# A linear-attention and MoE-style feed-forward kernel: attention products per head, in halves of the matrix array

## The chip, the cores and the metric

The kernel runs on one core of a Trainium2 chip. The metric is the device time of one execution in microseconds, 277.82 us in the median of three runs (277.59 to 278.0). The core has five engines that run side by side and are tied together by semaphores: TensorE (PE, matrix products; its weight loads are listed apart as PEld), VectorE (DVE), ScalarE (ACT), GpSimd (POOL) and SyncE (SP). In this kernel POOL and SP mostly issue transfers.

## The reference

For each of 8 batches and 8 heads, with 576 rows and a head width of 64, the reference forms `kv = k^T v` (64 x 64), then `out = q kv`, and divides each row of a head by its root mean square and scales it by `g_norm`. The heads are laid side by side, which gives x with 4608 rows (tokens) and 512 columns. Then

```
h = x @ w_in                                  # 4608 x 2048
g = max(h, 0) + alpha * min(h, 0)
y = g @ w_out                                 # 4608 x 512
```

The result is float32. The kernel computes its products on fp16 operands with fp32 sums.

## The kernel before

The 4608 tokens are cut into nine windows of 512. The main loop (L1010) runs over windows 1 to 8, and each pass has 16 units. A unit of pass w holds, in this order on PE: one group of the first product for a block of 128 hidden columns (`m1_group`, four products 128 x 512 into one PSUM bank, L487); seven products 128 x 256 of the second product of the window before (`prod_mm`, L665); and what `attention(w + 1, u)` adds, the attention of the window after, so that x of window w + 1 is ready when pass w + 1 starts. The order of all engines is written out by hand; each engine takes its instructions in program order.

The first product's bank is read twice: ACT makes `m_sb = relu(-h)` (L494) and then DVE makes `gt` from `m_sb` and the bank (L498). In passes 2 to 8 the first product has two banks in turn, tags h1 and h2, so the group of unit u + 2 may start only when `gt` of unit u is done. DVE also makes sums and differences of `gt` blocks (`s_sum`, L603 to L609, placed by `S_ROW`), because the second product is computed from seven block products in place of eight, and adds the partial results (`y_read`: p1, u2, u3, c11, c22, c21, c12).

From window 3 (`W_ROW`) the attention runs in rows. For each batch b from 3 to 7, `step_kv` multiplies k and v of a pair of heads at once: five products with 128 weight columns and 128 moving columns give a 128 x 128 block, of which only the two 64 x 64 blocks on the diagonal belong to a head; DVE multiplies by a mask and stores fp16 (L360). Four pairs make 20 products for a batch, placed in units 0, 0, 1, 1 of a pass (2, 2, 3, 3 in pass 2). Then, for each of the four row tiles of 128 tokens in the window, `rows_mm` multiplies the transposed q of a pair (the weights, 128 x 128) with the masked kv block (128 moving columns). Four products fill one bank of 512 columns; a tile that lies across two batches takes eight. There are 24 row tiles in windows 3 to 8, three of them across two batches. ACT squares the bank (`sq`, L444), DVE sums the squares per head (`ssq`, L450), ACT makes the reciprocal root (`rs`, L459), DVE scales (`norm`, L467) and SP transposes the rows into x by a transfer (L472).

These steps have fixed units: products of the tiles after units 2, 4, 6, 8; ssq in 4, 6, 8, 10; rs and norm in 5, 7, 9, 11; all one later in pass 2 (`ATT_ROW`, L975). SP also transposes q of the next batch in units 7, 9 and 11 (`QT_AT`), and ACT regroups k of the batch after (L177). The add u3 stands ahead of unit 10 and c22 ahead of unit 12 (`R_FIRST`). PSUM has eight banks, all in use: three of tags h, one y, one s, two o, one q. The kv blocks alternate between s and o; row tiles 0, 1 and 3 use o, tile 2 uses s.

Of the kernel before, what the change touches and what calls it, by code (L numbers as in the profile page):

```python
# [9 lines left out]
FP32 = mybir.dt.float32  # L10
FP16 = mybir.dt.float16
AF = mybir.ActivationFunctionType
ALU = mybir.AluOpType
# [4 lines left out]
def kernel(  # L18
# [11 lines left out]
    nc = tc.nc  # L30

    B, H, S, D = q.shape
# [3 lines left out]
    P = 128  # L36
    NPAIR = H // 2
    W = 512
# [15 lines left out]
    const_p = ctx.enter_context(tc.tile_pool(name="constp", bufs=1))  # L54
# [4 lines left out]
    attn_p = ctx.enter_context(tc.tile_pool(name="attn", bufs=2))  # L59
# [4 lines left out]
    ps_h = ctx.enter_context(tc.tile_pool(name="psh", bufs=1, space=bass.MemoryType.PSUM))  # L64
    ps_y = ctx.enter_context(tc.tile_pool(name="psy", bufs=1, space=bass.MemoryType.PSUM))
    ps_s = ctx.enter_context(tc.tile_pool(name="pss", bufs=1, space=bass.MemoryType.PSUM))
    ps_o = ctx.enter_context(tc.tile_pool(name="pso", bufs=2, space=bass.MemoryType.PSUM))
    ps_q = ctx.enter_context(tc.tile_pool(name="psq", bufs=1, space=bass.MemoryType.PSUM))

    ctx.enter_context(  # L70
        tc.manual_schedule(engines={ENG.PE, ENG.Activation, ENG.DVE, ENG.Pool, ENG.SP})
# [5 lines left out]
    def early_pair(eng, nm, tag):  # L77
# [14 lines left out]
            name=nc.get_next_instruction_name(),  # L92
# [9 lines left out]
    mask32 = const_p.tile([P, P], FP32, name="mask32")  # L102
# [7 lines left out]
    PAD = P // 2  # L110
    qt_sb = [const_p.tile([P, NPAIR, PAD + S + PAD], FP16, name=f"qt_sb{i}") for i in range(2)]
# [6 lines left out]
    for r in range(P // D):  # L118
        nc.sync.dma_start(
            out=alpha_row[NF : NF + 1, r * D : (r + 1) * D], in_=g_norm[:].unsqueeze(0)  # L120
# [6 lines left out]
    bufs = []  # L127
    for i in range(NBUF):
        t = {}
        for nm in ("k", "v", "q") if i < 2 else ("k", "v"):  # L130
            n = 1 if nm == "v" else T0 if i == 0 else NT
# [150 lines left out]


    qts, kvs, xts = {}, {}, {}

    def rows(b):
        return P0 if b == 0 else P

    def n_runs(b):
        return T0 if b == 0 else NT  # L290

    def pair_cols(b, nm, j):
        def f(t):
            n = rows(b)
            if nm == "v" and b == 0:
                h = 2 * j % HH
                return stages[b, nm, 2 * j // HH][0:n, h : h + 2, t, :]
            if nm == "v" and t < TPP:
                return stages[b, nm][:, 2 * j : 2 * j + 2, t, :]
            if nm == "v":  # L300
                return buf_of(b, nm)[0:n, 0, 2 * j : 2 * j + 2, :]
            return buf_of(b, nm)[0:n, t, 2 * j : 2 * j + 2, :]
        return f
# [44 lines left out]
    def step_kv(b, j, pool=(ps_s, "s")):  # L348
        ks, vs = pair_cols(b, "k", j), pair_cols(b, "v", j)
        kv_ps = pool[0].tile([P, P], FP32, name="kv_ps", tag=pool[1])  # L350
        for t in range(n_runs(b)):
            nc.tensor.matmul(  # L352
                out=kv_ps[:],
                lhsT=ks(t),
                rhs=vs(t),
                start=(t == 0),
                stop=(t == n_runs(b) - 1),
            )
        kvs[b, j] = attn_p.tile([P, P], FP16, name="kv_sb", tag=f"kv{j}")
        nc.vector.tensor_mul(out=kvs[b, j][:], in0=kv_ps[:], in1=mask32[:])  # L360


    ots = {}

    def step_ot(w, j, pool=None, parts=1):
        if pool is not None:
            ot_ps = pool[0].tile([P, W], FP32, name="ot_ps", tag=pool[1])
        else:
            ot_ps = ps_o.tile([P, W], FP32, name="ot_ps", tag="o")
        n0 = w * W  # L370
        while n0 < (w + 1) * W:
            b = n0 // S
            n1 = min((b + 1) * S, (w + 1) * W, n0 + W // parts)
            nc.tensor.matmul(  # L374
                out=ot_ps[:, n0 - w * W : n1 - w * W], lhsT=kvs[b, j][:],
                rhs=qts[b, j][:, n0 - b * S : n1 - b * S], start=True, stop=True,
            )
            n0 = n1
        sq = attn_p.tile([P, W], FP16, name="sq_sb")
        for c in col_parts(parts):  # L380
            nc.scalar.activation(out=sq[:, c], in_=ot_ps[:, c], func=AF.Square)
        ots[w, j] = (ot_ps, sq)
# [34 lines left out]
            xts[w] = xt_p.tile([P, NPAIR, W], FP16, name="xt")  # L417
        return xts[w][:, j, :]

    def rows_mm(w, i):  # L420
        n0 = w * W + i * P
        b, r = divmod(n0, S)
        pool, tag = (ps_s, "s") if i == 2 else (ps_o, "o")
        o_ps = pool.tile([P, W], FP32, name="or_ps", tag=tag)
        for j in range(NPAIR):
            cols = o_ps[:, j * P : (j + 1) * P]
            if r + P <= S:
                c = PAD + r
                nc.tensor.matmul(  # L429
                    out=cols, lhsT=qt_sb[b % 2][:, j, c : c + P], rhs=kvs[b, j][:],  # L430
                    start=True, stop=True,
                )
            else:
                assert r + PAD == S
                nc.tensor.matmul(
                    out=cols, lhsT=qt_sb[b % 2][:, j, S : S + P], rhs=kvs[b, j][:],
                    start=True, stop=False,
                )
                nc.tensor.matmul(
                    out=cols, lhsT=qt_sb[(b + 1) % 2][:, j, 0:P], rhs=kvs[b + 1, j][:],  # L440
                    start=False, stop=True,
                )
        sq = attn_p.tile([P, W], FP16, name="sq_sb")
        nc.scalar.activation(out=sq[:], in_=o_ps[:], func=AF.Square)  # L444
        ots[w, "r", i] = (o_ps, sq)

    def rows_ssq(w, i):
        o_ps, sq = ots.pop((w, "r", i))
        ssq = attn_p.tile([P, H], FP32, name="ssq_r")
        nc.vector.tensor_reduce(  # L450
            out=ssq[:], in_=sq[:].rearrange("p (h d) -> p h d", h=H),
            axis=mybir.AxisListType.X, op=ALU.add,
        )
        ots[w, "r", i] = (o_ps, ssq)

    def rows_rs(w, i):
        o_ps, ssq = ots.pop((w, "r", i))
        rstd = attn_p.tile([P, H], FP32, name="rstd_r")
        nc.scalar.activation(  # L459
            out=rstd[:], in_=ssq[:], func=AF.Abs_reciprocal_sqrt, bias=eps_t[:], scale=inv_d,  # L460
        )
        ots[w, "r", i] = (o_ps, rstd)

    def rows_norm(w, i):
        o_ps, rstd = ots.pop((w, "r", i))
        xr = attn_p.tile([P, H, D], FP16, name="x_rows", tag="rstd" if i % 2 else "x_rows")
        nc.vector.tensor_tensor(  # L467
            out=xr[:], in0=o_ps[:].rearrange("p (h d) -> p h d", h=H),
            in1=rstd[:].unsqueeze(2).to_broadcast([P, H, D]), op=ALU.mult,
        )  # L470
        xt_cols(w, 0)
        nc.sync.dma_start_transpose(  # L472
            out=xts[w][:, :, i * P : (i + 1) * P], in_=xr[:].rearrange("p h d -> p (h d)"),
        )

    gts = {}
# [135 lines left out]
    part = {}  # L612
# [124 lines left out]
    Q_POOL, S_POOL, O_POOL = (ps_q, "q"), (ps_s, "s"), (ps_o, "o")  # L737
# [230 lines left out]
            ATT_1.setdefault(at, []).append((what, j))  # L968
    ATT = {"t": step_t, "kv": step_kv, "ot": step_ot, "ssq": step_ssq}

    def row_kv(w, j):
        step_kv(w, j, O_POOL if j % 2 else S_POOL)

    ATT_ROW = {}
    for first, kv_at, d in ((True, (2, 2, 3, 3), 1), (False, (0, 0, 1, 1), 0)):  # L975
        at_row = {}
        for what, ats in (
            ("kv", kv_at), ("mm", (2 + d, 4, 6, 8)), ("ssq", (4, 6, 8, 10)),
            ("rs", (5, 7, 9, 11)), ("norm", (5, 7, 9, 11)),
        ):  # L980
            for j, at in enumerate(ats):
                at_row.setdefault(at if what == "kv" else at + d, []).append((what, j))
        ATT_ROW[first] = at_row
    ROWS = {"kv": row_kv, "mm": rows_mm, "ssq": rows_ssq, "rs": rows_rs, "norm": rows_norm}
    QT_AT = {False: {7: (0,), 9: (1,), 11: (2, 3, 4)}, True: {8: (0,), 10: (1,), 12: (2, 3, 4)}}

    def attention(w, u):
        if W_ROW <= w < NW:
            for what, j in ATT_ROW[w == W_ROW].get(u, ()):
                if what != "kv" or w < B:  # L990
                    ROWS[what](w, j)
            if w + 1 < B:
                dma_t(w + 1, QT_AT[w == W_ROW].get(u, ()))
        elif w < NW:
            for what, j in (ATT_1 if w == 2 else ATT_AT).get(u, ()):
                if what == "t" and w >= B_NAT:
                    continue
                if w < B or what in ("ot", "ssq"):
                    if w == 2 and what in ("kv", "ssq"):
                        pool = Q_POOL if j % 2 == 0 else S_POOL  # L1000
                        (step_kv if what == "kv" else step_ssq)(w, j, pool)
                    else:
                        ATT[what](w, j)
# [1 line left out]
    REG_AT = {9 + 2 * j: (("k", j),) for j in range(NPAIR)}  # L1005

    Y3_AT = [(13, 13), (13, 13), (13, 13), (13, 14), (14, 14), (14, 15), (15, 15), (15, 15), (15, 15), (15, 15), (15, 15), (15, 15), (15, 15), (15, 15), (15, 16), (16, 16)]
    REG_2 = {0: (("k", 0), ("k", 1)), 1: (("k", 2),), 2: (("k", 3),)}

    for w in range(1, NW):  # L1010
        if w + 2 < B:
# [50 lines left out]
    w = NW - 1  # L1062
# [56 lines left out]
```

## Time and profile before

| | |
|---|---|
| median of three runs | 277.82 us |
| profiled execution, first to last instruction (span) | 275.2 us |
| what lies around the span, by the difference to the median | 2.6 us |
| PE, PEld, DVE, ACT, POOL busy | 269.1, 176.1, 231.2, 154.9, 86.3 us |
| TensorE clock granted | 1.000 |
| passes with row attention (2 to 7) | about 66 to 233 us of the span |

The page gives no time of the profiled execution other than its span, so the 2.6 us are the median of the runs less that span. Matrix products overlap in the array: a record of one product is its time from start to end, and the rate is read from the distance between starts. Starts in the timeline are microseconds from the start of the span.

### The profile page before, as it was taken

How to read it: one execution, taken by the hardware profiler on the slowest of the kernel's cores; microseconds unless marked ns; L12 is line 12 of the kernel's file. 1: busy time of each engine (PE TensorE's matmuls, PEld its weight loads, DVE VectorE, ACT ScalarE, POOL GpSimd, SP SyncE). 2: the span in 40 equal slices, each digit the busy share in tenths (PEclk: the TensorE clock that was granted, in tenths of full speed). 3: DMA queues.
4: the chain of work that ended last, by engine and by line, in shares of the span. 5: the costliest groups of instructions: out<-in, count | busy, mean ns of one | idle time of the engine just before them, and what ended most of it. 6: DMA issues, size and time to landing. Idle time of an engine off the chain costs nothing.

```text
span 275.2 us, 5282 instructions
## 1 busy us (share of the span) xinstructions
PE 269.1 (98%) x1973; PEld 176.1 (64%) x1973; DVE 231.2 (84%) x451; ACT 154.9 (56%) x286; POOL 86.3 (31%) x123
## 2 busy tenths in 40 slices
PE   7899999999999999999999999999999999999995
PEld 3454454555776776676667766676667666666794
DVE  6659758799789979997999799978997999887863
ACT  3568446799989746644665456645545553444210
POOL 8853463660912338127322641100111011000200
PEclk9999999999999999999999999999999999999999
DMA  8999999999999849997984799520322032201223
GB/s 160 197 203 198 197 202 189 215 132 182 129 172 129 124 91 138 174 204 100 173 155 120 114 166 175 118 87 2 76 76 79 6 83 67 76 2 38 72 84 114
DMA packets 87341, 34.53 MB, mean 125 GB/s; under 512 B 58884, under 2 KB 85652, under 8 KB 87316
## 3 DMA queue, kind: packets, MB, share of 16 engines
q0 software_dynamic: 58064, 24.35, 68.3%
q1 hardware_dynamic: 28212, 8.83, 16.9%
q10 hardware_dynamic: 1040, 1.02, 1.2%
q8 instruction: 15, 0.25, 0.4%
q14 instruction: 10, 0.08, 0.1%
HBM read 36.71 MB, written 9.44 MB: 168 GB/s over the span
## 4 chain that ended last, share of the span: by engine, by line
PE 87%; DMA 10%; POOL 1%; issue 1%; DVE 0%; POOLq 0%
PE h_ps L487 38%; PE yY L665 15%; PE yX L665 10%; PE yZ L665 10%; DMA qst<-in_q_dram 8%; PE y L519 4%; PE kv_ps L352 3%; DMA w_in_sb<-in_moe_w_in_dram 2%; PE h_ps L510 2%; PE or_ps L429 2%; PE qt_ps L308 1%; PE ssq_ps L397 1%; PE yZ L660 1%; PE ot_ps L374 1%; POOL vst L142 0%
## 5 line engine op out<-in xcount | busy, mean ns | idle before, releaser
L487 PE MATMUL h_ps<-xt,w_in_sb 128*128 128x512 f16 x544 | 136.8, 379 | 0.0
L494 ACT ACTIVATE m_sb<-h_ps 128x512 f32<-128x512 f32 x144 | 86.1, 598 | 79.8 <-PE h_ps L487 69.6
L498 DVE SCALAR_TENSOR_TENSOR gt<-m_sb,beta_sb,h_ps 128x512 f16<-128x512 f32 x144 | 106.4, 745 | 23.6 <-ACT m_sb L494 21.8
L487 PEld LDWEIGHTS <-w_in_sb 128*128 128x128 f16 x544 | 51.6, 98 | 38.9
L530 POOL DMA_DIRECT2D out_dram<-y_sb x36 | 22.6, 630 | 134.8 <-DVE y_sb L709 43.7
L665 PEld LDWEIGHTS <-s 128*128 128x128 f16 x496 | 48.5, 98 | 19.1
L665 PEld LDWEIGHTS <-gt 128*128 128x128 f16 x384 | 37.3, 98 | 14.0
L665 PE MATMUL yY<-wsum,s 128*128 128x256 f16 x256 | 36.3, 273 | 0.0
L665 PE MATMUL yX<-w_out_sb,gt 128*128 128x256 f16 x256 | 36.1, 273 | 0.0
L159 POOL DMA_DIRECT2D qst<-in_q_dram x20 | 17.7, 923 | 1.8 <-DMA vst<-in_v_dram 1.8
L665 PE MATMUL yY<-wsum,gt 128*128 128x256 f16 x128 | 17.6, 273 | 0.0
L444 ACT ACTIVATE sq_sb<-or_ps 128x512 f16<-128x512 f32 x24 | 14.3, 597 | 5.7 <-PE or_ps L429 4.6
L665 PE MATMUL yZ<-wsum,s 128*128 128x256 f16 x120 | 16.7, 273 | 0.0
L665 PE MATMUL yZ<-w_out_sb,s 128*128 128x256 f16 x120 | 16.7, 273 | 0.0
L467 DVE TENSOR_TENSOR x_rows<-or_ps,rstd_r 128x512 f16<-128x512 f32 x24 | 16.4, 685 | 0.0
L450 DVE TENSOR_REDUCE ssq_r<-sq_sb 128x8 f32<-128x512 f16 x24 | 16.3, 680 | 0.0
L519 PE MATMUL y<-w_out_sb,gt 128*128 128x512 f16 x64 | 15.9, 379 | 0.0
L605 DVE TENSOR_TENSOR s<-s,gt 128x512 f16<-128x512 f16 x32 | 13.5, 422 | 0.5
L603 DVE TENSOR_TENSOR s<-gt 128x512 f16<-128x512 f16 x32 | 13.5, 420 | 0.0
L609 DVE TENSOR_TENSOR s<-gt,s 128x512 f16<-128x512 f16 x32 | 13.3, 420 | 0.0
L697 DVE TENSOR_TENSOR u<-yY,p 128x512 f32<-128x512 f32 x16 | 11.0, 684 | 1.9 <-PE yY L665 1.7
L607 DVE TENSOR_TENSOR s<-gt 128x512 f16<-128x512 f16 x32 | 12.6, 418 | 0.0
(88 smaller groups left out, 269.9 us busy)
## 6 DMA issues: line engine op xcount, KB each, us to landing
out_dram<-y_sb POOLq DMA_DIRECT2D x16, 256.0 KB, 2.7
kst<-in_k_dram POOLq DMA_DIRECT2D x7, 512.0 KB, 7.0
vst<-in_v_dram POOLq DMA_DIRECT2D x6, 512.0 KB, 9.2
qst<-in_q_dram POOLq DMA_DIRECT2D x20, 128.0 KB, 6.8
w_out_sb<-in_moe_w_out_dram POOLq DMA_DIRECT2D x8, 256.0 KB, 11.6
out_dram<-y_sb SPq DMA_DIRECT2D x5, 256.0 KB, 2.3
w_in_sb<-in_moe_w_in_dram POOLq DMA_DIRECT2D x2, 512.0 KB, 10.6
qst<-in_q_dram POOLq DMA_DIRECT2D x2, 512.0 KB, 12.2
```

Of the source, the lines that this page charges most:

```text
L159: nc.gpsimd.dma_start(out=st[:, t, :, :], in_=srcs["q"][b, :, t * P : (t + 1) * P, :].rearrange("h p d -> p h d"),)
L444: nc.scalar.activation(out=sq[:], in_=o_ps[:], func=AF.Square)
L450: nc.vector.tensor_reduce(out=ssq[:], in_=sq[:].rearrange("p (h d) -> p h d", h=H), axis=mybir.AxisListType.X, op=ALU.add,)
L467: nc.vector.tensor_tensor(out=xr[:], in0=o_ps[:].rearrange("p (h d) -> p h d", h=H), in1=rstd[:].unsqueeze(2).to_broadcast([P, H, D]), op= ...
L487: nc.tensor.matmul(out=h_ps[:], lhsT=w_in_blk(c, g), rhs=xts[w][:, c, :], start=(c == 0), stop=(c == NC - 1),)
L494: nc.scalar.activation(out=m_sb[:], in_=h_ps[:], func=AF.Relu, scale=-1.0)
L498: nc.vector.scalar_tensor_tensor(out=gts[w, i][:, r, :], in0=m_sb[:], scalar=beta_sb[:, g : g + 1], in1=h_ps[:], op0=ALU.mult, op1=ALU.add,)
L519: nc.tensor.matmul(out=y[:], lhsT=gt_cols(w, g, a * P, (a + 1) * P), rhs=w_out_blk(g), start=(g == 0), stop=(g == NF - 1),)
L530: engs[store_turn[0] % len(engs)].dma_start(out=dst, in_=src)
L603: nc.vector.tensor_add(out=t[:], in0=a21, in1=a22)
L605: nc.vector.tensor_sub(out=t[:], in0=sums[w, 1, k][:], in1=a11)
L665: nc.tensor.matmul(out=bank, lhsT=lhs, rhs=rhs, start=fresh, stop=(c == NK - 1), skip_group_check=True,)
```

## The change

Kv products of batches 3 to 7 are formed per head. The five products of a pair become ten, each with the 64 columns of one head as weights and 64 moving columns; head 0 of the pair writes PSUM partitions 0 to 63 and head 1 partitions 64 to 127, so each uses one half of the array's columns. All four pairs of a batch go into one bank of tag s, in one run of 40 products in unit 0 (unit 2 in pass 2). Two DVE copies of 64 partitions x 256 elements replace the four masked multiplies, and write only the diagonal blocks of one of two fixed tiles `kv_masked`, whose other blocks were left zero by batches 0 to 2, which still use the masked multiply.

Row products are formed per head as well: the weights are 64 rows of transposed q with 128 columns, so each uses one half of the array's rows; the moving operand is the 64 x 64 block of kv. Two row tiles are done in one run, 16 products (24 with a tile across two batches) into a tile of two banks, one bank for each of the two heads of a pair. The runs stand after units 2 and 7 (4 and 8 in pass 2). The tile of two banks takes the place of the two o banks and has one buffer, so the products of tiles 2 and 3 come after the norm of tile 1. The following steps move: ssq from units 4, 6, 8, 10 to 3, 4, 8, 9; rs from 5, 7, 9, 11 to 4, 5, 9, 10; norm from 5, 7, 9, 11 to 4, 6, 9, 11. The last regroup of k for batch 3 moves from unit 2 to unit 1 of pass 2.

```diff
-    ps_o = ctx.enter_context(tc.tile_pool(name="pso", bufs=2, space=bass.MemoryType.PSUM))
     ps_q = ctx.enter_context(tc.tile_pool(name="psq", bufs=1, space=bass.MemoryType.PSUM))
+    o_scope = ctx.enter_context(ExitStack())
+    ps_o = o_scope.enter_context(tc.tile_pool(name="pso", bufs=2, space=bass.MemoryType.PSUM))
+    row_pool = []
...
+    kv_masked = [const_p.tile([P, NPAIR, P], FP16, name=f"kv_masked{i}") for i in range(2)]
...
-        kvs[b, j] = attn_p.tile([P, P], FP16, name="kv_sb", tag=f"kv{j}")
-        nc.vector.tensor_mul(out=kvs[b, j][:], in0=kv_ps[:], in1=mask32[:])
+        kvs[b, j] = kv_masked[b % 2][:, j, :]
+        nc.vector.tensor_mul(out=kvs[b, j], in0=kv_ps[:], in1=mask32[:])
...
-    def rows_mm(w, i):
-        n0 = w * W + i * P
-        b, r = divmod(n0, S)
-        pool, tag = (ps_s, "s") if i == 2 else (ps_o, "o")
-        o_ps = pool.tile([P, W], FP32, name="or_ps", tag=tag)
-        for j in range(NPAIR):
-            cols = o_ps[:, j * P : (j + 1) * P]
-            if r + P <= S:
-                c = PAD + r
-                nc.tensor.matmul(
-                    out=cols, lhsT=qt_sb[b % 2][:, j, c : c + P], rhs=kvs[b, j][:],
-                    start=True, stop=True,
-                )
...
-        sq = attn_p.tile([P, W], FP16, name="sq_sb")
-        nc.scalar.activation(out=sq[:], in_=o_ps[:], func=AF.Square)
-        ots[w, "r", i] = (o_ps, sq)
+    def rows_mm(w, i0):
+        if not row_pool:
+            o_scope.close()
+            row_pool.append(
+                ctx.enter_context(tc.tile_pool(name="psr", bufs=1, space=bass.MemoryType.PSUM))
+            )
+        o_ps = row_pool[0].tile([P, 2, 2, NPAIR, D], FP32, name="or_ps", tag="o")
+        for i in (i0, i0 + 1):
+            b, r = divmod(w * W + i * P, S)
+            for j in range(NPAIR):
+                if r + P <= S:
+                    steps = ((b, PAD + r),)
+                else:
+                    assert r + PAD == S
+                    steps = ((b, S), (b + 1, 0))
+                for n, (bb, c) in enumerate(steps):
+                    for h in range(2):
+                        part = slice(h * D, (h + 1) * D)
+                        nc.tensor.matmul(
+                            out=o_ps[:, h, i - i0, j, :],
+                            lhsT=qt_sb[bb % 2][part, j, c : c + P],
+                            rhs=kvs[bb, j][part, part],
+                            start=(n == 0), stop=(n == len(steps) - 1), skip_group_check=True,
+                        )
+        for i in (i0, i0 + 1):
+            sq = attn_p.tile([P, 2, NPAIR, D], FP16, name="sq_sb")
+            nc.scalar.activation(out=sq[:], in_=o_ps[:, :, i - i0], func=AF.Square)
+            ots[w, "r", i] = (o_ps[:, :, i - i0], sq)
...
-        xr = attn_p.tile([P, H, D], FP16, name="x_rows", tag="rstd" if i % 2 else "x_rows")
+        xr = attn_p.tile([P, NPAIR, 2, D], FP16, name="x_rows", tag="rstd" if i % 2 else "x_rows")
         nc.vector.tensor_tensor(
-            out=xr[:], in0=o_ps[:].rearrange("p (h d) -> p h d", h=H),
-            in1=rstd[:].unsqueeze(2).to_broadcast([P, H, D]), op=ALU.mult,
+            out=xr[:].rearrange("p j h d -> p h j d"), in0=o_ps,
+            in1=rstd[:].unsqueeze(3).to_broadcast([P, 2, NPAIR, D]), op=ALU.mult,
         )
...
-    def row_kv(w, j):
-        step_kv(w, j, O_POOL if j % 2 else S_POOL)
+    def row_kv(b):
+        kv_ps = ps_s.tile([P, NPAIR, D], FP32, name="kv_ps", tag="s")
+        for j in range(NPAIR):
+            ks, vs = pair_cols(b, "k", j), pair_cols(b, "v", j)
+            for t in range(n_runs(b)):
+                for i in range(2):
+                    rows_i = slice(i * D, (i + 1) * D)
+                    nc.tensor.matmul(
+                        out=kv_ps[rows_i, j, :], lhsT=ks(t)[:, i, :], rhs=vs(t)[:, i, :],
+                        start=(t == 0), stop=(t == n_runs(b) - 1), skip_group_check=True,
+                    )
+        for i in range(2):
+            rows_i = slice(i * D, (i + 1) * D)
+            nc.vector.tensor_copy(
+                out=kv_masked[b % 2][rows_i, :, rows_i], in_=kv_ps[rows_i, :, :]
+            )
+        for j in range(NPAIR):
+            kvs[b, j] = kv_masked[b % 2][:, j, :]
 
     ATT_ROW = {}
-    for first, kv_at, d in ((True, (2, 2, 3, 3), 1), (False, (0, 0, 1, 1), 0)):
-        at_row = {}
+    for first, kv_at, d in ((True, 2, 1), (False, 0, 0)):
+        at_row = {kv_at: [("kv", None)]}
         for what, ats in (
-            ("kv", kv_at), ("mm", (2 + d, 4, 6, 8)), ("ssq", (4, 6, 8, 10)),
-            ("rs", (5, 7, 9, 11)), ("norm", (5, 7, 9, 11)),
+            ("mm", (2 + d, None, 7, None)), ("ssq", (3, 4, 8, 9)),
+            ("rs", (4, 5, 9, 10)), ("norm", (4, 6, 9, 11)),
         ):
...
-    REG_2 = {0: (("k", 0), ("k", 1)), 1: (("k", 2),), 2: (("k", 3),)}
+    REG_2 = {0: (("k", 0), ("k", 1)), 1: (("k", 2), ("k", 3))}
```

More of the change, by code (lines that the diff above doesn't have):

```diff
@@ L374, in step_ot @@
             nc.tensor.matmul(
-                out=ot_ps[:, n0 - w * W : n1 - w * W], lhsT=kvs[b, j][:],
+                out=ot_ps[:, n0 - w * W : n1 - w * W], lhsT=kvs[b, j],
                 rhs=qts[b, j][:, n0 - b * S : n1 - b * S], start=True, stop=True,
@@ L418, in xt_cols @@
         return xts[w][:, j, :]
-    def rows_mm(w, i):
-        n0 = w * W + i * P
-        b, r = divmod(n0, S)
-        pool, tag = (ps_s, "s") if i == 2 else (ps_o, "o")
-        o_ps = pool.tile([P, W], FP32, name="or_ps", tag=tag)
-        for j in range(NPAIR):
-            cols = o_ps[:, j * P : (j + 1) * P]
-            if r + P <= S:
-                c = PAD + r
-                nc.tensor.matmul(
-                    out=cols, lhsT=qt_sb[b % 2][:, j, c : c + P], rhs=kvs[b, j][:],
-                    start=True, stop=True,
-                )
[L433 to L442, printed above, removed]
-        sq = attn_p.tile([P, W], FP16, name="sq_sb")
-        nc.scalar.activation(out=sq[:], in_=o_ps[:], func=AF.Square)
-        ots[w, "r", i] = (o_ps, sq)
+    def rows_mm(w, i0):
[26 more added lines that the diff above has]
+            ots[w, "r", i] = (o_ps[:, :, i - i0], sq)
@@ L447, in rows_ssq @@
     def rows_ssq(w, i):
         o_ps, sq = ots.pop((w, "r", i))
-        ssq = attn_p.tile([P, H], FP32, name="ssq_r")
+        ssq = attn_p.tile([P, 2, NPAIR], FP32, name="ssq_r")
         nc.vector.tensor_reduce(
-            out=ssq[:], in_=sq[:].rearrange("p (h d) -> p h d", h=H),
+            out=ssq[:].rearrange("p h j -> p (h j)"),
+            in_=sq[:].rearrange("p h j d -> p (h j) d"),
             axis=mybir.AxisListType.X, op=ALU.add,
@@ L457, in rows_rs @@
         o_ps, ssq = ots.pop((w, "r", i))
-        rstd = attn_p.tile([P, H], FP32, name="rstd_r")
+        rstd = attn_p.tile([P, 2, NPAIR], FP32, name="rstd_r")
         nc.scalar.activation(
@@ L472, in rows_norm @@
         nc.sync.dma_start_transpose(
-            out=xts[w][:, :, i * P : (i + 1) * P], in_=xr[:].rearrange("p h d -> p (h d)"),
+            out=xts[w][:, :, i * P : (i + 1) * P], in_=xr[:].rearrange("p j h d -> p (j h d)"),
         )
@@ L969 @@
     ATT = {"t": step_t, "kv": step_kv, "ot": step_ot, "ssq": step_ssq}
-    def row_kv(w, j):
-        step_kv(w, j, O_POOL if j % 2 else S_POOL)
+    def row_kv(b):
[16 more added lines that the diff above has]
+            kvs[b, j] = kv_masked[b % 2][:, j, :]
     ATT_ROW = {}
-    for first, kv_at, d in ((True, (2, 2, 3, 3), 1), (False, (0, 0, 1, 1), 0)):
-        at_row = {}
+    for first, kv_at, d in ((True, 2, 1), (False, 0, 0)):
+        at_row = {kv_at: [("kv", None)]}
         for what, ats in (
-            ("kv", kv_at), ("mm", (2 + d, 4, 6, 8)), ("ssq", (4, 6, 8, 10)),
-            ("rs", (5, 7, 9, 11)), ("norm", (5, 7, 9, 11)),
+            ("mm", (2 + d, None, 7, None)), ("ssq", (3, 4, 8, 9)),
+            ("rs", (4, 5, 9, 10)), ("norm", (4, 6, 9, 11)),
         ):
             for j, at in enumerate(ats):
-                at_row.setdefault(at if what == "kv" else at + d, []).append((what, j))
+                if at is None:
+                    continue
+                at_row.setdefault(at + d, []).append((what, j))
         ATT_ROW[first] = at_row
-    ROWS = {"kv": row_kv, "mm": rows_mm, "ssq": rows_ssq, "rs": rows_rs, "norm": rows_norm}
+    ROWS = {"mm": rows_mm, "ssq": rows_ssq, "rs": rows_rs, "norm": rows_norm}
     QT_AT = {False: {7: (0,), 9: (1,), 11: (2, 3, 4)}, True: {8: (0,), 10: (1,), 12: (2, 3, 4)}}
@@ L989, in attention @@
             for what, j in ATT_ROW[w == W_ROW].get(u, ()):
-                if what != "kv" or w < B:
+                if what != "kv":
                     ROWS[what](w, j)
+                elif w < B:
+                    row_kv(w)
             if w + 1 < B:
```

## The prediction

> **What bounds the kernel now.** I read the page first, for the busy shares, the slices and the chain that ended last.
>
> ```profile
> span 275.2 us, 5282 instructions
> PE 269.1 (98%) x1973; PEld 176.1 (64%) x1973; DVE 231.2 (84%) x451; ACT 154.9 (56%) x286; POOL 86.3 (31%) x123
> PE   7899999999999999999999999999999999999995
> DVE  6659758799789979997999799978997999887863
> PE 87%; DMA 10%; POOL 1%; issue 1%; DVE 0%; POOLq 0%
> ```
>
> PE is busy in every slice after the start, and the chain runs through PE for 87% of the span. So a microsecond added to PE's stream or taken from it is a microsecond of time, as long as no other engine holds PE back. DVE is the candidate: 9 in many slices, 84% on average.
>
> Next, the groups of instructions with their shapes kept apart, for what the change touches.
>
> ```profile
> L352 PE MATMUL kv_ps<-vst,ksb 128*128 128x128 f16 x112 | 9.4, 219 | 0.0
> L429 PE MATMUL or_ps<-kv_sb,qt_sb 128*128 128x128 f16 x84 | 8.1, 219 | 0.0
> L429 PEld LDWEIGHTS <-qt_sb 128*128 128x128 f16 x84 | 6.5, 98 | 0.5
> L450 DVE TENSOR_REDUCE ssq_r<-sq_sb 128x8 f32<-128x512 f16 x24 | 16.3, 680 | 0.0
> L360 DVE TENSOR_TENSOR kv_sb<-kv_ps,mask 128x128 f16<-128x128 f32 x32 | 8.1, 286 | 3.4 <-PE kv_ps L352 3.4
> ```
>
> The 219 ns of a product is its latency. Its rate is in the timeline of PE, in unit 0 of pass 5 (columns: start, length, what, count):
>
> ```profile
> 151.76 0.39 PE L352 MATMUL kv_ps<-vst,ksb 128*128 128x128 f16 x4
> 151.99 0.22 PE L352 MATMUL kv_ps<-vsb,ksb 128*128 128x128 f16 x1
> 152.04 0.39 PE L352 MATMUL kv_ps<-vst,ksb 128*128 128x128 f16 x4
> 152.26 0.22 PE L352 MATMUL kv_ps<-vsb,ksb 128*128 128x128 f16 x1
> 152.32 1.03 PE L487 MATMUL h_ps<-xt,w_in_sb 128*128 128x512 f16 x4
> ```
>
> Ten products take 152.32 - 151.76 = 0.56 us: 56 ns each, with a weight load (98 ns by its own record) for every one, wholly hidden. In the same timeline seven products of 256 columns take 0.77 us (110 ns each) and four of 512 take 0.86 us (216 ns), so a unit without attention is 1.63 us. Nothing stands between them.
>
> Last, DVE around units 9 to 12 of the same pass, and PE's start of unit 12.
>
> ```profile
> 168.49 0.75 DVE L498 SCALAR_TENSOR_TENSOR gt<-m_sb,beta_sb,h_ps 128x512 f16<-128x512 f32 x1
> 169.15 0.42 DVE L609 TENSOR_TENSOR s<-gt,s 128x512 f16<-128x512 f16 x1
> 169.49 0.69 DVE L467 TENSOR_TENSOR x_rows<-or_ps,rstd_r 128x512 f16<-128x512 f32 x1
> 170.09 0.68 DVE L697 TENSOR_TENSOR u<-yY,p 128x512 f32<-128x512 f32 x1
> 170.68 0.74 DVE L498 SCALAR_TENSOR_TENSOR gt<-m_sb,beta_sb,h_ps 128x512 f16<-128x512 f32 x1
> 171.34 0.68 DVE L450 TENSOR_REDUCE ssq_r<-sq_sb 128x8 f32<-128x512 f16 x1
> 171.68 1.03 PE L487 MATMUL h_ps<-xt,w_in_sb 128*128 128x512 f16 x4
> ```
>
> The starts follow each other without a gap from 168.49. The gt of unit 10 ends at 170.68 + 0.74 = 171.42 and frees the bank that unit 12 takes at 171.68: 0.26 us to spare. Two units on (gt of unit 12 from 174.12, 0.74 long; unit 14 at 174.93) only 0.07 us are left. PE and DVE are balanced here, and a wait of PE is not seen yet.
>
> **Part 1, twice as many products of half the size.** Before: 5 batches x 20 = 100 kv products and 24 x 4 + 3 x 4 = 108 row products, 208 x 56 ns = 11.65 us, all on the path. After: 200 and 216, 416 with 64 moving columns. No 64-column pair of weight load and product in a run is in this trace. The three rates above fit 2.5 ns + 0.417 ns a column, so 64 columns are 29.2 ns. Lower end: the two halves run side by side, 14.6 ns each, 6.1 us: -5.6 us. Halves one after the other at 29.2 ns: 12.1 us, +0.5 us. Upper end: no pair of load and product passes faster than the 56 ns of the nearest run, 23.3 us: +11.65 us. A halved array that gains nothing from halving would be odd, and one that loses nothing between loads would be too, so I take the middle of 14.6 and 29.2, 21.9 ns: 9.1 us, -2.5 us.
>
> A rule that speaks against this is on the page "TensorEngine Tiling (Array Packing)" of the Trainium skill, section Restrictions and Gotchas: column tiling excludes the fast weight load. With the load time that "TensorE: Matmul & The Clock Gate", section LDWEIGHTS, gives (columns divided by 1.2 in ns, 53 ns for 64 columns), 200 kv loads that are not hidden in each other would be an estimated 10.7 us in place of the 5.6 us that 100 kv products take here, so +5.1 us from kv alone. The trace has 56 ns for a whole pair with 128 weight columns, which is below that formula's 107 ns, and shows no load in a half array.
>
> **Part 2, changes of shape.** PE's stream now changes between full-array and half-array products: 5 runs of kv and 12 of rows, 17 x 2 = 34 changes. The trace has no such change. If the products under way must end first, a change exposes what a dense run hides, 219 - 56 = 163 ns; if the first weights also can't be loaded ahead, another 98 ns, 261 ns in all. Lower end 0, nothing to gain: 0 to 34 x 0.261 = 8.9 us. Neither row is nearer; I take the middle, 0.13 us each: +4.4 us. No work covers it, as PE is the bound.
>
> The page "TensorEngine Tiling (Array Packing)", section Key Properties, says that changing the tiling mode drains the engine, with no figure; no run here shows it yet. Read as 163 ns each it would be an estimated 5.5 us in place of the 4.4.
>
> **Part 3, the moved DVE work.** In passes 3 to 7 ssq of tile 3 moves from behind the gt of unit 10 to ahead of it (unit 9). It holds DVE for 171.93 - 171.34 = 0.59 us (next start). From the fence: gt of unit 10 starts at 170.68 + 0.59 = 171.27, ends at 172.01, and with some 0.06 us for the release unit 12 starts at 172.07 in place of 171.68: PE stands for 0.4 us. The stretch is measured from the start of unit 9, so a faster or slower row run ahead of it changes nothing. By unit 11 the order of DVE is as before, so unit 14 gains slack. Five passes: 2.0 us.
>
> Earlier, ssq of tile 0 (unit 4 to 3), ssq of tile 1 (6 to 4) and norm of tile 0 (5 to 4) pile up in units 3 and 4. With u the start of unit 3: gt 1.69 to 2.35, two sums to 3.02, ssq to 3.62, gt of unit 4 to 4.28, sum, ssq and norm to 5.8, gt of unit 5 to 6.55, release 6.6; unit 7 wants its bank at 4 x 1.63 = 6.52. That is at the edge, 0 to 0.1 us a pass; I take 0 and keep 0.5 us for the upper end. In pass 2 ACT also scales w_in (0.61 us a unit), the steps are one unit later, and ssq of tile 3 and norm of tile 2 both come ahead of the gt of unit 11, which started at 87.55 and now starts near 88.26; unit 13 at 88.90 then waits some 0.2 us, with 0.1 at unit 8: 0.3. Sum of the part: +2.3 us; lower end 0 (the slack is larger than read), upper end 3.3 us.
>
> **Part 4, the rest.** The kv copies: two of 64 x 256 in place of four multiplies at 286 ns (1.14 us). The nearest row of 256 f32 elements is the final add at 422 ns, so 0.84 us or, at 286 ns each, 0.57 us: DVE gains 0.3 to 0.6 us a batch in units 0 and 1, where it sat idle for 0.29 us and 0.70 us: 0 on the path. All 40 kv products now stand at once in unit 0; the later first product moves by the same amount, nothing waits. The last regroup of k for pass 2 (0.6 us on ACT, one unit earlier) delays m_sb of unit 2 by 0.5 us; its gt then ends near 72.4, and unit 4 starts at 73.14: 0. Two squares (0.6 us each, 0.5 us apart) in a row end 1.0 us after the row run, before m_sb of the next unit is due 1.06 us after its start: 0; in pass 2 w_in delays this by some 0.2 us, covered by the slack in gt. The norm has the same 512 elements in another order, 685 ns; if order costs a tenth, 0.07 us more stands ahead of unit 12, 0.4 us in all. SP's transposes follow the norms: tile 0, 1 one unit earlier, 2 and 3 as before. The q transposes of unit 7 stand on SP behind the row run of that unit, which reads the same buffer; they are wanted after unit 2 of the next pass, 11 units or 18 us later, and land in 2.4 us: 0. POOL's loads of the next k and v wait for regroup and kv, both no later than before: 0.
>
> **Sum.** -2.5 + 4.4 + 2.3 = +4.2 us on the span of 275.2, 279.4 us; with the 2.6 us that lie around it, 282.0 us against the median of 277.82.
>
> **Rivals.** Faster: the halves run side by side (14.6 ns), changes of shape are free, DVE's stall stays: -5.6 + 2.3 = -3.3 us, 274.5 us. For it: each half uses its own rows or columns and PSUM bank or partitions, and 56 ns shows loads hidden well. Against: 34 changes and half-size loads that nothing here prices. It decides from a change of shape below (5.6 - 2.3) / 34 = 0.097 us. Chance 0.22.
>
> Load-bound: each small pair takes the 56 ns that a large one takes, +11.65 + 4.4 + 2.3 = +18.3 us, 296.1 us; if for kv alone (200 x 56 = 11.2, rows at 21.9 = 4.7, together 15.9 or +4.3 us), 4.3 + 4.4 + 2.3 = +11.0, 288.8 us. For it: loads double in number while the product that hides each is halved. Against: the load's own limit is only known to be at most 56 ns. Chance 0.13.
>
> A wash: side by side, and changes near 0.1 us, so that what the halves win goes into changes and DVE: -5.6 + 3.4 + 2.3 = +0.1, 277.9 us. Chance 0.08.
>
> **How the numbers follow.** The forecast, 282.0 us, has 0.57, with its own range of 278.4 to 287.5. About 0.2% (0.55 us) is what this measurement can tell from no change. Slower: forecast and load-bound, 0.57 + 0.13 less 0.02 that fall elsewhere, 0.68; same 0.08; faster 0.22 + 0.02 = 0.24. The range leaves out about a tenth at each side: 275.3 (the inner part of the faster rival) to 289.5 (load-bound for kv inside, for all outside).
>
> **What would show it.** Part 1: starts of the half products in the timeline, 15, 22, 29 or 56 ns apart, and the length of a kv run, before 1.12 us for 20 products. Part 2: a gap or late start between the last product of 256 columns and the first half product, and back. Part 3: PE's first product of unit 12 late by 0.4 us, released by gt, with ssq, norm, u3, gt in that order on DVE. The prediction is wrong if runs of kv and rows are much shorter than 1.1 and 0.45 us with changes included, or if unit 12 is not late.

## The result and the profile after

The changed kernel takes 282.64 us in the median of four runs (282.2 to 282.73), the kernel before 277.75 us (277.59 to 278.0, four runs). The ratio is 1.0183 with a 95% interval of 1.0168 to 1.0197: slower by 4.9 us. The forecast was 282.0 us. The sum was close; its terms were not, and the experiments below find which ones hold. One execution of the kernel of the third experiment took 728.66 us, in the slow state, and stands in no median and no ratio below.

From the page of the changed kernel, the lines that answer to those of before:

```profile
span 280.7 us, 5677 instructions
PE 269.2 (96%) x2181; PEld 170.0 (61%) x2181; DVE 230.5 (82%) x441; ACT 154.6 (55%) x286; POOL 86.8 (31%) x123
PE 59%; DVE 20%; DMA 10%; ACT 5%; issue 5%; POOL 1%; POOLq 0%
```

PE's share of the chain that ended last fell from 87% to 59%, and DVE, with less work than before, now has 20% of it. Busy shares alone would not say so: PE's fell from 98% to 96%, DVE's from 84% to 82%. The list of PE's waits (total, times, longest) names the main one:

```profile
PE yY L671 <- DVE u L703: 3.2, 5, 0.7
```

It did not exist before. Half-array products, in the timeline of PE, pass 5, unit 0 (start, length, what, count):

```profile
153.94 0.49 PE L671 MATMUL yX<-w_out_sb,gt 128*128 128x256 f16 x3
154.37 0.32 PE L984 MATMUL kv_ps<-vst,ksb 128*64 128x64 f16 x8
...
154.54 0.29 PE L984 MATMUL kv_ps<-vst,ksb 128*64 128x64 f16 x8
154.67 0.20 PE L984 MATMUL kv_ps<-vsb,ksb 128*64 128x64 f16 x2
154.70 0.29 PE L984 MATMUL kv_ps<-vst,ksb 128*64 128x64 f16 x8
...
154.99 0.20 PE L984 MATMUL kv_ps<-vsb,ksb 128*64 128x64 f16 x2
155.12 1.04 PE L493 MATMUL h_ps<-xt,w_in_sb 128*128 128x512 f16 x4
```

Ten half products take 154.70 - 154.54 = 0.16 us, 16 ns each. Their single starts come in pairs, one for each of two heads: 3 to 4 ns within a pair, 28 ns from the second of a pair to the next, so two heads pass side by side. The three products from 153.94 on take 0.33 us, so the first kv product could have started at 154.27 and starts 0.10 us later; the last pair of kv products starts at 154.99, 0.13 us ahead of the full-array product at 155.12, where 0.03 us would do: another 0.10 us. The whole stretch, 154.27 to 155.12, is 0.85 us against 1.12 us for the 20 products of before. A run of two row tiles takes about as long as before:

```profile
157.84 0.71 PE L671 MATMUL yY<-wsum,s 128*128 128x256 f16 x5
158.48 0.41 PE L441 MATMUL or_ps<-kv_masked,qt_sb 64*128 64x64 f16 x16
158.82 1.04 PE L493 MATMUL h_ps<-xt,w_in_sb 128*128 128x512 f16 x4
```

Between the same marks (158.39 to 158.82) it is 0.43 us against 2 x 0.225. A run with a tile across two batches, 24 products, is 0.55 us against 0.67.

Then DVE and PE of the same pass, units 3 to 6 (DVE) and the seven products 128 x 256 of unit 6 (PE):

```profile
160.54 0.75 DVE L504 SCALAR_TENSOR_TENSOR gt<-m_sb,beta_sb,h_ps 128x512 f16<-128x512 f32 x1 [1.00 <-ACT m_sb L500]
161.20 0.76 DVE L613 TENSOR_TENSOR s<-gt 128x512 f16<-128x512 f16 x2
161.87 0.68 DVE L455 TENSOR_REDUCE ssq_r<-sq_sb 128x8 f32<-128x512 f16 x1
162.47 0.74 DVE L504 SCALAR_TENSOR_TENSOR gt<-m_sb,beta_sb,h_ps 128x512 f16<-128x512 f32 x1
163.12 0.42 DVE L613 TENSOR_TENSOR s<-gt 128x512 f16<-128x512 f16 x1
163.46 0.68 DVE L455 TENSOR_REDUCE ssq_r<-sq_sb 128x8 f32<-128x512 f16 x1
164.06 0.68 DVE L473 TENSOR_TENSOR x_rows<-or_ps,rstd_r 128x512 f16<-128x512 f32 x1
164.65 0.74 DVE L504 SCALAR_TENSOR_TENSOR gt<-m_sb,beta_sb,h_ps 128x512 f16<-128x512 f32 x1
165.31 0.68 DVE L703 TENSOR_TENSOR u<-yY,p 128x512 f32<-128x512 f32 x1
```

```profile
164.58 0.82 PE L671 MATMUL yX<-w_out_sb,gt 128*128 128x256 f16 x6
166.04 0.27 PE L671 MATMUL yY<-wsum,s 128*128 128x256 f16 x1 [0.65 <-DVE u L703]
```

DVE runs without a gap from 160.54 to the add u2, which reads the bank of yY and ends at 165.99. The last product of unit 6 begins the next sum in that bank and starts at 166.04. Six products from 164.58 take 0.66 us, so it could have started at 165.24: 0.80 us lost (the record calls 0.65 idle, because the products ahead of it still drain). The same 0.80 us stand in each of passes 3 to 7. In the kernel before, the same add and the same products stood like this:

```profile
162.19 0.68 DVE L697 TENSOR_TENSOR u<-yY,p 128x512 f32<-128x512 f32 x1
162.33 0.82 PE L665 MATMUL yX<-w_out_sb,gt 128*128 128x256 f16 x6
162.98 0.27 PE L665 MATMUL yY<-wsum,s 128*128 128x256 f16 x1
```

There u2 ended at 162.87, 0.11 us before the product started on time.

Units 11 and 12 of the same pass, DVE then PE:

```profile
172.55 0.68 DVE L455 TENSOR_REDUCE ssq_r<-sq_sb 128x8 f32<-128x512 f16 x1
173.14 0.68 DVE L473 TENSOR_TENSOR x_rows<-or_ps,rstd_r 128x512 f16<-128x512 f32 x1
173.74 0.68 DVE L703 TENSOR_TENSOR u<-yY,p 128x512 f32<-128x512 f32 x1
174.34 1.39 DVE L504 SCALAR_TENSOR_TENSOR gt<-m_sb,beta_sb,h_ps 128x512 f16<-128x512 f32 x2
```

```profile
173.97 0.49 PE L671 MATMUL yZ<-wsum,s 128*128 128x256 f16 x3
174.47 0.60 PE L671 MATMUL yY<-wsum,gt 128*128 128x256 f16 x4
175.13 1.02 PE L493 MATMUL h_ps<-xt,w_in_sb 128*128 128x512 f16 x4
```

The product after u3 could start at 174.30 and starts at 174.47, when u3 has ended (174.42); unit 12 could start at 174.91 and starts at 175.13, when gt of unit 10, the first of the two in the last DVE line, has ended (174.34 + 0.74 = 175.08). That is 0.17 + 0.22 = 0.39 us a pass. No bracket marks it, because the records of the products ahead reach over the gap; it shows only in the distance of starts.

In pass 2 PE is late in other places: 0.08 us at unit 8 and 0.30 us ahead of the row run of that unit, which needs the tile of two banks that the norm of tile 1 frees:

```profile
82.76 0.41 PE L441 MATMUL or_ps<-kv_masked,qt_sb 64*128 64x64 f16 x16 [0.23 <-DVE x_rows L473]
```

Also in pass 2, the kv products of the last pair start at 71.67 where 71.50 would do, and the run takes 1.03 us in place of 0.85. The regroup of k that the change moved up, on ACT, ends at 71.61. No run was made for this wait alone; in the second experiment below, where the regroup and the products of the last pair keep their units of before, no kv run is longer than the others.

### The profile page after: what moved, and what is told of

Same layout as the page of the kernel before. It is cut to its first block, busy times and chain, and to the rows that moved or that the text cites. A ratio compares the mean times of both kernels' runs of the same rounds, so it can differ in the third digit from the quotient of the medians.

```text
span 280.7 us, 5677 instructions
## 1 busy us (share of the span) xinstructions
PE 269.2 (96%) x2181; PEld 170.0 (61%) x2181; DVE 230.5 (82%) x441; ACT 154.6 (55%) x286; POOL 86.8 (31%) x123
## 4 chain that ended last, share of the span: by engine, by line
PE 59%; DVE 20%; DMA 10%; ACT 5%; issue 5%; POOL 1%; POOLq 0%
PE h_ps L493 25%; PE yY L671 10%; DMA qst<-in_q_dram 8%; DVE gt L504 7%; PE yX L671 6%; PE yZ L671 6%; PE y L525 4%; DVE ssq_r L455 3%; DVE x_rows L473 3%; ACT m_sb L500 3%; DVE u L703 2%; DMA w_in_sb<-in_moe_w_in_dram 2%; ACT sq_sb L449 2%; PE h_ps L516 2%; DVE s L613 2%
## 5 line engine op out<-in xcount | busy, mean ns | idle before, releaser
L449 ACT ACTIVATE sq_sb<-or_ps 128x512 f16<-128x512 f32 x24 | 13.0, 594 | 0.8 <-PE or_ps L441 0.2
```

What stands on the lines that cost most here:

```text
L449: nc.scalar.activation(out=sq[:], in_=o_ps[:, :, i - i0], func=AF.Square)
```

## The experiments

The theory (A): half-array products gain on PE, and what is lost is lost to the new places of DVE's row steps, which hold back the adds u2 and u3 and a gt. The rival (B): the half-array runs themselves, with their changes of shape, are the loss. A third reading, kept for the last runs: DVE is simply full in these passes, and a step moved away only moves the wait. Within each of the two groups of four below the runs share a chip and the runs of the kernel before: 277.84 us for the first group, 277.51 us for the second.

**Only kv in halves.** The kernel before, with the changed `row_kv`, the two tiles `kv_masked` and the regroup of k; row products and their steps untouched.

```diff
-    def row_kv(w, j):
-        step_kv(w, j, O_POOL if j % 2 else S_POOL)
+    def row_kv(b):
+        kv_ps = ps_s.tile([P, NPAIR, D], FP32, name="kv_ps", tag="s")
...
-    for first, kv_at, d in ((True, (2, 2, 3, 3), 1), (False, (0, 0, 1, 1), 0)):
-        at_row = {}
+    for first, kv_at, d in ((True, 2, 1), (False, 0, 0)):
+        at_row = {kv_at: [("kv", None)]}
```

> Only the kv products are in column halves, 40 in one run in unit 0 with two copies; row products, PSUM tiles and all DVE steps are as before. Theory A (half-array runs gain, the moved DVE steps lose): a kv run with both changes of shape took 0.85 us in the changed kernel's timeline (last full product to next full product) against 1.12 us before, so 5 x -0.27 = -1.3 us, 276.4 us, and no wait of PE for u or gt in unit 6 or 12. Theory B (the half-array runs or their changes of shape are the loss): at 277.8 us or above.

Measured: 276.39 us, ratio 0.9951 (0.9932 to 0.9969), faster than before by 1.4 us. PE has no wait for u or gt in the row passes. Theory A holds for the kv halves, B falls for them.

**The same in two runs.** Pairs 0 and 1 after unit 0, pairs 2 and 3 after unit 1.

```diff
-        kv_ps = ps_s.tile([P, NPAIR, D], FP32, name="kv_ps", tag="s")
-        for j in range(NPAIR):
+        pool, tag = O_POOL if pairs[0] else S_POOL
+        kv_ps = pool.tile([P, NPAIR, D], FP32, name="kv_ps", tag=tag)
+        for j in pairs:
...
-        at_row = {kv_at: [("kv", None)]}
+        at_row = {kv_at: [("kv", (0, 1))], kv_at + 1: [("kv", (2, 3))]}
```

> As the kernel with kv alone in halves, but the 40 products stand in two runs of 20, in units 0 and 1 (2 and 3 in pass 2), each with its own bank and two copies of half the width. It adds five pairs of changes of shape and nothing else on PE. Theory A with changes at 0.09 to 0.10 us each: 5 x 0.19 = +0.95 us on the kernel with kv alone, about 277.4 us. If a change of shape were free in time and only a gap in the records: the same as kv alone. Theory B: further above before.

Measured: 277.27 us, ratio 0.9981 (0.9968 to 0.9993). Ten more changes of shape cost 277.27 - 276.39 = 0.88 us, 0.09 us each, against 0.09 to 0.10 in the timeline; each of the twelve runs lies above all six of the kernel with one run. So the gaps in the records are time. The page "TensorEngine Tiling (Array Packing)" of the Trainium skill, section Key Properties, says that a change of tiling mode drains the engine; that each change costs time here, 0.09 us, agrees with it.

**Full-array products in the changed order.** One bank for each of two row tiles, 4 or 8 products a tile; 20 products a batch for kv; everything else as changed.

```diff
-                for i in range(2):
-                    rows_i = slice(i * D, (i + 1) * D)
-                    nc.tensor.matmul(
-                        out=kv_ps[rows_i, j, :], lhsT=ks(t)[:, i, :], rhs=vs(t)[:, i, :],
+                nc.tensor.matmul(
+                    out=kv_ps[:, j, :], lhsT=ks(t), rhs=vs(t),
...
-                    for h in range(2):
-                        part = slice(h * D, (h + 1) * D)
-                        nc.tensor.matmul(
-                            out=o_ps[:, h, i - i0, j, :],
-                            lhsT=qt_sb[bb % 2][part, j, c : c + P],
-                            rhs=kvs[bb, j][part, part],
+                    nc.tensor.matmul(
+                        out=o_ps[:, i - i0, j, :, :],
+                        lhsT=qt_sb[bb % 2][:, j, c : c + P], rhs=kvs[bb, j],
```

> The order of the changed kernel (one kv run, two row tiles at a time in a tile of two banks, ssq, rs and norm where the change put them), but with the full-array products of before: 20 a batch for kv, 4 or 8 a row tile. Theory A: the waits of PE for DVE stay (some 0.65 us in unit 6 and 0.4 us in units 11 and 12 of each of five passes, less in pass 2), and the gain of the halves, 5 x 0.27 + 12 x 0.02 = 1.6 us, is lost too: 282.6 + 1.6 = 284.2 us. Theory B: without half-array runs the loss is gone, about 277.8 us.

Measured: 286.19 us, ratio 1.0297 (1.0265 to 1.0329). There is no half-array product in this kernel, and it is the slowest of all: B falls. It is 2.0 us above the figure that A gave. Two lines of its PE timeline (passes 3 and 5) show part of that:

```profile
97.01 0.38 PE L514 MATMUL h_ps<-xt,w_in_sb 128*128 128x128 f16 x4 [0.92 <-DMA xt<-x_rows]
...
168.78 0.27 PE L669 MATMUL yY<-wsum,s 128*128 128x256 f16 x1 [0.75 <-DVE u L701]
```

Once, PE waited for the last transposed rows of x (0.92 us); and the lost time per pass was 0.9 us in unit 6 and 0.46 us in units 11 and 12, against 0.80 and 0.39, five times some 0.18 us. With 0.9 these make 1.8 of the 2.0 us. The longer wait in unit 6 starts at the squares of the early row run: they start 0.20 us after the first product of unit 3 (161.67 against 161.47) where the changed kernel has 0.11 us (158.93 against 158.82), and m_sb, gt and u2 follow later by as much.

**The order mended.** All half-array products of the change, and other units for the row steps: the first line below is for pass 2, the second for passes 3 to 7.

```diff
-            ("mm", (2 + d, None, 7, None)), ("ssq", (3, 4, 8, 9)),
-            ("rs", (4, 5, 9, 10)), ("norm", (4, 6, 9, 11)),
+        (True, 2, ((3, None, 8, None), (3, 4, 8, 9), (4, 5, 9, 10), (5, 6, 10, 12))),
+        (False, 0, ((1, None, 7, None), (2, 3, 7, 8), (3, 4, 8, 9), (5, 5, 9, 10))),
```

(The four tuples are products, ssq, rs and norm.)

> All half-array products of the changed kernel, with the row steps placed anew: from pass 3, row products after units 1 and 7, ssq in 2, 3, 7, 8, rs in 3, 4, 8, 9, norm in 5, 5, 9, 10 (both early norms behind the add u2 of unit 5, ssq of tiles 0 and 1 where DVE sat idle in units 2 and 3, ssq of tile 3 two gt ahead of unit 12); pass 2 one or two units later. Theory A: PE no longer waits for u in unit 6 nor for u and gt in units 11 and 12; what is left is the gain of the halves, 1.6 us below before: 276.2 us. Theory B, or DVE being full whatever the order: above 278 us, with waits in other units.

Measured: 276.35 us, ratio 0.9948 (0.9928 to 0.9968), where 276.2 us was expected. DVE in units 5 and 6 of pass 5, then PE:

```profile
161.16 0.75 DVE L504 SCALAR_TENSOR_TENSOR gt<-m_sb,beta_sb,h_ps 128x512 f16<-128x512 f32 x1 [0.31 <-ACT m_sb L500]
161.82 0.68 DVE L703 TENSOR_TENSOR u<-yY,p 128x512 f32<-128x512 f32 x1
162.43 1.28 DVE L473 TENSOR_TENSOR x_rows<-or_ps,rstd_r 128x512 f16<-128x512 f32 x2
```

```profile
161.90 0.82 PE L671 MATMUL yX<-w_out_sb,gt 128*128 128x256 f16 x6
162.56 0.27 PE L671 MATMUL yY<-wsum,s 128*128 128x256 f16 x1
```

u2 ends at 162.50, the product starts at 162.56, on time; the same reduces and norms are still done, before and behind it. DVE even waits 0.31 us for ACT ahead of this gt. So DVE was not full: the changed kernel and this one give DVE the same work, and with it in another order PE has none of the waits of units 6, 11 and 12 any more.

**One half of the mending at a time.** First only the late half: ssq of tile 3 back behind the gt of unit 10.

```diff
-            ("mm", (2 + d, None, 7, None)), ("ssq", (3, 4, 8, 9)),
-            ("rs", (4, 5, 9, 10)), ("norm", (4, 6, 9, 11)),
+        (False, 0, ((2, None, 7, None), (3, 4, 8, 10), (4, 5, 9, 11), (4, 6, 9, 11))),
```

> The changed kernel with one step put back from pass 3 on: ssq of tile 3 in unit 10, behind the gt of that unit, with its rs in unit 11; all else as changed. In the changed kernel PE stands 0.17 us ahead of the first product that follows u3 (unit 11) and 0.22 us ahead of unit 12, 0.39 us in each of five passes. If that reduce alone makes these two waits: 282.6 - 2.0 = 280.7 us, both waits gone, the one in unit 6 as it was. If DVE is simply full: the waits move on and the time stays near 282.6 us.

Measured: 280.72 us, ratio 1.0115 (1.0093 to 1.0137). Expected 280.7. The timeline has no late start in units 11 and 12 any more, and 0.81 us in unit 6 of each of the five passes as in the changed kernel. Then only the early half:

```diff
-            ("mm", (2 + d, None, 7, None)), ("ssq", (3, 4, 8, 9)),
-            ("rs", (4, 5, 9, 10)), ("norm", (4, 6, 9, 11)),
+        (False, 0, ((1, None, 7, None), (2, 3, 8, 9), (3, 4, 9, 10), (5, 5, 9, 11))),
```

> The changed kernel with the early half placed anew from pass 3 on: products of tiles 0 and 1 after unit 1, ssq in 2 and 3, both norms in unit 5 behind the add u2; the late half and pass 2 as changed. In the changed kernel PE stands 0.80 us in unit 6 of five passes until u2 has read the bank of yY. If what stands ahead of u2 makes that wait: 282.6 - 4.0 = 278.6 us, with the waits of units 11 and 12 still there. If DVE is simply full: at most a part of it comes back.

Measured: 278.26 us, ratio 1.003 (1.0018 to 1.0042). Expected 278.6. The wait in unit 6 is gone and the 0.17 + 0.22 us of units 11 and 12 stand in all five passes. The two waits are independent, and the steps put ahead of u2 and of the gt of unit 10 make them. By the ratios to the kernel before (1.0183 for the changed kernel, 1.0115, 1.003, and 0.9948 with both mended), since these runs were taken at different times, the late half is worth 1.9 us, the early half 4.2 us and both with pass 2 6.5 us; the lost starts in the timeline make 2.0 and 4.0 us.

**What the halves are worth without the waits.** The mended order with row products of the full array, and with all products of the full array (edits as in the third experiment).

> The kernel with the mended order, with kv in column halves but row products of the full array (4 a tile, 8 across two batches, each tile in one bank). Half rows cost 216 x 0.0157 us and 24 changes of shape at 0.093 us, 5.6 us, against 108 x 0.056 = 6.05 us, so 0.4 us slower than the mended kernel, about 276.8 us, if the halves in rows are worth anything; 276.3 us if nothing.

> The mended order with full-array products throughout, none in halves. Theory A: no waits of PE, and PE's products are those of the kernel before, so 277.8 us, which makes the difference to the mended kernel (276.35 us), 1.5 to 1.7 us, the whole worth of the halves. If the mended order itself were worth something beside the halves: below 277.3 us.

Measured: 276.45 us, ratio 0.9965 (0.9948 to 0.9982), with rows full; 277.9 us, ratio 1.0016 (1.0002 to 1.0029), with all full. In the mended order, kv in halves is worth 277.9 - 276.45 = 1.45 us, and all halves, by the ratios 1.0016 and 0.9948 of the two groups, about 0.7% or 1.9 us. The times can't tell whether the row halves add the 0.4 us that was expected: 0.9965 and 0.9948 come from different groups and their intervals overlap. The timelines can: from the last full product ahead of each run to the first behind it, the twelve row runs together take 6.22 us with full products and 5.80 us in halves, 0.4 us less. Each sum includes a wait of about 0.2 us in pass 2; without any wait the halves are 5.58 us, against 6.04 us in the kernel before. For kv the same sums are 5.58 us before and 4.24 us in halves, plus 0.19 us of wait in pass 2. So the halves are worth 1.8 us on PE, of which the mended kernel keeps 1.4. The order itself gains nothing: with full products it is no faster than before, and by the ratio 1.0016 rather 0.4 us slower.

Three kernels are clearly faster than both: kv alone in halves, the mended order, and the mended order with full row products, at 276.35 to 276.45 us.

## Why the prediction was right, and where not

The forecast of 282.0 us missed by 0.6 us. Its sign was right, and so were DVE holding PE back at unit 12 and changes of shape on the path. That the sum came so close is luck: the +4.2 us came out of terms that were off in both directions:

| term | forecast, us | measured, us |
|---|---|---|
| 1, half products | -2.5 (21.9 ns each) | -5.0 (416 x 16 ns = 6.7 against 11.65) |
| 2, changes of shape | +4.4 (0.13 each) | +3.2 (34 x 0.095) |
| 3, DVE, units 11 and 12 | +2.0 | +2.0 (5 x 0.39) |
| 3, DVE, unit 6 (forecast: unit 7) | 0, upper end 0.5 | +4.0 (5 x 0.80) |
| 3, DVE, pass 2 | +0.3 (0.1 at unit 8, 0.2 at unit 13) | +0.4 (0.08 at unit 8, 0.30 ahead of its row run, 0.02 at unit 13) |
| 4, kv run of pass 2 | 0 | +0.2 |
| sum | +4.2 | +4.8 |

The time moved by 4.9 us. The profiled executions differ by 5.5 us in span, of which 0.5 us are there before pass 2 begins (first full unit at 67.66 against 67.14), where the row attention has not started. The 2.6 us that were put around the span of before mix two executions: in the runs on record the time is 1.85 to 2.09 us above the span of the same run, so the profiled execution of before was some 0.6 us faster than the median. The forecast doesn't suffer from it, since it adds 4.2 us to the median.

**Part 1** took the middle between halves in turn and side by side; side by side was right, for rows and columns alike. The bound was in the text, the choice was mis-sized by 2.5 us. Row halves pass a little faster, 14.5 ns; how the time of the runs is split between the first two rows of the table is good to some 0.3 us, their sum, 9.8 us against 11.6, is read from starts. The rival "load-bound" fell: no pair took 56 ns. The weight-load estimate worked out in the prediction from the two pages of the skill (53 ns for 64 columns, "TensorE: Matmul & The Clock Gate", section LDWEIGHTS) does not show in the rate: 16 ns a product with its load, though a load's own record is 112 ns.

**Part 2** said 0 to 0.26 us and took 0.13; it is 0.095, in the timeline and by the run that added ten. Parts 1 and 2 together are -1.8 us where +1.9 was forecast: the sign of the PE side was wrong. The sign that was named for this, kv runs much shorter than 1.1 us, did show: 0.85 us. The faster rival's condition, a change below 0.097 us, lies at the edge of what was measured (0.09 to 0.10), and yet the kernel is clearly slower, because that condition was worked out with 2.3 us for DVE. The wash, with a chance of 0.08, had the PE side nearly right (-5.6 + 3.4 = -2.2 us) and missed by DVE's wait.

**Part 3** is the step that failed. It followed the chain gt, bank of the first product, for units 5 and 7, and found 0 to 0.1 us. It stopped at that gt. The add u2 right behind it is in no sum, and who waits for it was not asked: the add empties the bank of yY, into which the last product of unit 6 starts a new sum. The trace of before shows how tight that was: u2 ended at 162.19 + 0.68 = 162.87 and that product started at 162.98. From the start of unit 3, u2 now ends 0.66 us later (165.99 - 158.82 = 7.17 us against 162.87 - 156.36 = 6.51), behind a reduce and a norm more, less DVE's idle time there; and the product wants its bank 0.20 us sooner (6.42 us against 6.62), because the row run behind unit 4 no longer stands ahead of it. Of these 0.86 us the 0.11 to spare covered only 0.06, since the product follows the add by 0.05: 0.80 us. The working up to that gt was good (5.83 us measured for its start, 5.8 forecast). For units 11 and 12 the same chain, gt behind a reduce of 0.59 us, was worked out to 0.4 us and measured at 0.39, though 0.17 of it is taken through u3 and the yY bank rather than through gt. In pass 2 the size came out by luck: the 0.2 us forecast for unit 13 were 0.02, and the 0.30 us ahead of the row run, which waits for the norm of tile 1 because its two-bank tile has one buffer, was not forecast.

**Part 4** held but for one wait: two kv copies at 418 ns each (0.84 us forecast as the upper of two), the norm in the new layout 680 ns against 685, squares 594 against 597, and none of that reached the path. The regroup of k moved up in pass 2 was followed to m_sb and gt only; the kv products of the last pair, which read what it writes and now stand in the same run, start 0.17 us late, and the run is 0.19 us longer than the others.

So the result fell in the forecast's own range, but two errors stood against each other: 3.7 us of gain not believed (parts 1 and 2) and 4.3 us of waiting not seen (parts 3 and 4).

## What to carry to other kernels

Half-array products passed at 1.75 times the rate here (2 x 16 ns against 56), but every run pays for going in and out; it pays only in long runs (40 products saved 0.27 us, 24 products 0.12 us, 16 products 0.01 us). In a kernel whose engines are both near full, place a moved step by asking for each instruction behind it which buffer it frees and who writes there next; one late add cost 4.0 us where the halves had gained 1.8. When a change is slower, separate its parts before dropping it: the same products in another order are faster than the kernel before.

## What was not expected of the hardware

Half-array products of 64 moving columns passed at 16 ns each for column halves (160 ns for ten) and at 14.5 ns for row halves, with a weight load for every one, while one full-array product of 128 columns, which does the work of two, takes 56 ns. A change of shape costs 0.09 to 0.10 us in each direction, less than the 0.163 us by which a full product's latency exceeds its distance to the next. A late start of PE of some 0.2 us can be missing from the list of waits although it costs its full length: the 0.17 + 0.22 us of units 11 and 12 are in no wait of PE's list, and came back as 1.9 us when the reduce ahead of them was moved.
